# Attention in a fused attention and MLP kernel: from half-group steps to whole groups, prepared two ahead

## The chip, the cores and the metric

One Trainium2 chip, one core. The metric is the device time of one execution in microseconds (us), lower is better; the time before is the median of three runs.

## The reference

Attention over 2 sequences, 8 heads, 768 positions, head size 64. A query sees the first 4 keys (the sink) and the last 128. The result, 1536 tokens by 512, goes through two MLPs.

```python
scores = scale * np.matmul(q, k.transpose(0, 1, 3, 2))
keep = is_sink | in_window            # pos < n_sink, or 0 <= rel < window
scores = np.where(keep, scores, -1000000000.0)
a = np.exp(scores - np.max(scores, axis=-1, keepdims=True))
a = a / (np.sum(a, axis=-1, keepdims=True) + 1e-09)
x = np.matmul(a, v)                   # then heads side by side
x = (silu(x @ w_gate) * (x @ w_val)) @ w_out          # MLP 1: 512 -> 1536 -> 512
h = x @ w_in                                           # MLP 2: 512 -> 2048 -> 512
x = (np.maximum(h, 0) + alpha * np.minimum(h, 0)) @ w2_out
```

The MLP weights arrive as 64-bit floats.

## The kernel before

**Groups.** Attention is cut into 24 groups: one sequence, one pair of heads, two blocks of 128 queries (`i0` = 0, 2 or 4; `Group`, L143). Eight groups fill one token pass of 512 columns, so there are three passes. The first eight groups have `i0` = 0 and need no sink columns; the other sixteen do. A group goes through these steps:

- `load`, `load_v` (L164, L176): DMAs of its keys, queries and values, and of 32 sink keys when `i0` = 2, all issued by SyncE's queue (SP).
- `prep` (L189): TensorE (PE) transposes two or three key blocks (L206), the sink keys (L208) and two query blocks (L217) into PSUM; ScalarE (ACT) copies them to the tile `th` (L199), in two copies for a sink group.
- `scores(t)` for each of its two query blocks (L235): score matmuls (L256); VectorE (DVE) merges the two window blocks into one (L260) and adds the mask and takes the row maximum (L262, read back as `nb`); ACT does the exponential with a row sum (L266).
- `norm` (L279): DVE takes the reciprocal of the sums (L282, L283), GpSimd (POOL) multiplies (L291, L311).
- `flip(t)` (L313): PE transposes the probabilities (L323, L336); ACT (L327, L337) or DVE (L329) copies them out.
- `values` (L339): matmuls with the values (L354) and the sink values (L359); ACT and DVE split the result in two halves `xh`, `xl` (L823, L824).

**Weights.** `Stream` (L537) loads one 128-wide strip of weights at a time (512 KB, `w_raw`, 2 buffers) and converts it: ACT reads the high words (`w_m`, L574), DVE does three integer operations (L576, L579, L582) into `w`, ACT writes the upper part `wh` (L591), DVE the lower `wl` (L592). There are 68 strips. 13 converted strips have a place during attention, 6 more after it. A strip is loaded when one before it has been converted.

**MLP 1** runs in units of one chunk (4 strips each of gate, value and out) and one token pass: matmuls `pg`, `pv` (L642 to L644) and `po` (L706 to L708), all 128x128 by 128x512, 144 in a unit. The first two units (chunk 0, passes 0 and 1) are woven into the attention of the later passes; the third and all others come after it.

**Order.** The code is emitted in the order of `attention` (L366): half a group per step, the values three steps later (`LAG`), `prep` one group ahead. A scheduler of the language then sets the final order on each engine at build time; each engine runs its list strictly in that order. All PSUM tiles share 8 banks.

Of the kernel before, what the change touches and what calls it, by code (L numbers as in the profile page):

```python
# [7 lines left out]
F32 = mybir.dt.float32  # L8
# [28 lines left out]
RB = 2  # L37
LAG = 3
VB = 4
ORDER = ((0, 3), (1, 2), (4, 5))  # L40
TICK0 = 14
# [91 lines left out]
def attention_pools(nc, tc, ctx, g):  # L133
    for nm, bufs in (("raw_p", 2), ("tr_p", 2), ("pr_p", 3), ("pt_p", 2), ("st_p", 4)):
        setattr(g, nm, ctx.enter_context(tc.tile_pool(name=nm, bufs=bufs)))
    g.nb = g.const.tile([P, B * H * NQ], F32, name="nb")
    g.wsum = g.const.tile([P, NW], F32, name="wsum")
    g.ksr = g.const.tile([NPAIR * SINK, 2, D], F32, name="ksr")
    g.vsr = g.const.tile([4 * SINK, NPAIR, NG, 2 * D], F32, name="vsr")
    nc.gpsimd.memset(g.vsr, 0.0)  # L140


class Group:  # L143
    def __init__(self, nc, g, q, k, v, b, hp, i0, put, cs, blk):
# [3 lines left out]
        self.rows = slice(hp * SINK, (hp + 1) * SINK)  # L148
# [5 lines left out]
        self.kpos, c = [], 0  # L154
        for t in range(self.nk):
            self.kpos.append(c)
            c += P
            if t == 1 and self.sink:
                self.spos = c
                c += SINK  # L160
        self.kw = c
        self.whole = True

    def load(self):  # L164
        nc, p = self.nc, self.g.raw_p
        b, h0, j0, nk, i0 = self.b, self.h0, self.j0, self.nk, self.i0
        qr = p.tile([P, NG, 2, D], F32, tag="qr", name="qr")
        kr = p.tile([P, NK, 2, D], F32, tag="kr", name="kr")
        for e in range(2):
            nc.sync.dma_start(out=kr[:, :nk, e], in_=self.k[b, h0 + e, j0 * P:(j0 + nk) * P, :].rearrange("(t p) d -> p t d", p=P))  # L170
            nc.sync.dma_start(out=qr[:, :, e], in_=self.q[b, h0 + e, i0 * P:(i0 + NG) * P, :].rearrange("(t p) d -> p t d", p=P))
        if i0 == NG:
            nc.sync.dma_start(out=self.g.ksr[self.rows], in_=self.k[b, h0:h0 + 2, 0:SINK, :].rearrange("h p d -> p h d"))
# [15 lines left out]
    def prep(self):  # L189
        nc, g, nk = self.nc, self.g, self.nk  # L190
        n = NK * P + SINK + NG * P
        if self.whole:
            self.th = g.tr_p.tile([P, n], F32, tag="th", name="th")
        else:
            self.th = g.tr_p.tile([P, n], F32R, tag="th", name="th")
            self.tl = g.tr_p.tile([P, n], F32R, tag="tl", name="tl")

        def evac(ps, c, w):
            nc.scalar.activation(self.th[:, c:c + w], ps[:, :w], AF.Copy)  # L199
            if not self.whole:  # L200
                nc.vector.tensor_tensor(out=self.tl[:, c:c + w], in0=ps[:, :w], in1=self.th[:, c:c + w], op=ALU.subtract)

        self.qpos = q0 = self.kw
        ps = g.ps_t.tile([P, 512], F32, tag="ps", name="ps_k")
        for t in range(nk):
            nc.tensor.transpose(ps[:, self.kpos[t]:self.kpos[t] + P], self.kr[:, t], g.ident)  # L206
        if self.sink:
            nc.tensor.transpose(  # L208
                ps[:, self.spos:self.spos + SINK], g.ksr[self.rows].rearrange("p e d -> p (e d)"), g.ident[self.rows, self.rows]
            )  # L210
        if self.kw + NG * P > 512:
            evac(ps, 0, self.kw)
            yield 110 * nk + 60
            ps = g.ps_t.tile([P, 512], F32, tag="ps", name="ps_q")
            q0 = 0
        for t in range(NG):
            nc.tensor.transpose(ps[:, q0 + t * P:q0 + (t + 1) * P], self.qr[:, t], g.ident)  # L217
        if q0:
            evac(ps, 0, q0 + NG * P)
        else:  # L220
            evac(ps, self.kw, NG * P)
        yield 110 * NG
# [12 lines left out]
    def scores(self, t):  # L235
# [13 lines left out]
        qs, ks = slice(self.qpos + t * P, self.qpos + (t + 1) * P), slice(lo, lo + first + w)  # L249
        terms = [(self.th, self.th)]  # L250
        if not self.whole:
            terms += [(self.tl, self.th), (self.th, self.tl)]
        for z, (qx, kx) in enumerate(terms):
            for e in range(2):
                r = slice(e * D, (e + 1) * D)
                nc.tensor.matmul(pss[e][:, :first + w], qx[r, qs], kx[r, ks], start=(z == 0), stop=(z == len(terms) - 1))  # L256
# [108 lines left out]

def attention(groups, begin):  # L366
# [11 lines left out]
    for c in groups[0].prep():  # L378
        yield c, None
    for x in range(NG * n + LAG + 1):  # L380
        gi, t = divmod(x, NG)
        if x < NG * n:
            groups[gi].scores(t)
            yield 600, None
        y = x - LAG - 1
        if y >= 0 and y % NG == NG - 1:
            for c in groups[y // NG].values():
                yield c, None
            yield 0, groups[y // NG]
        y = x - LAG  # L390
        if 0 <= y < NG * n:
            groups[y // NG].flip(y % NG)
            yield 500, None
        if x < NG * n and t == NG - 1:
            groups[gi].norm()
            yield 0, None
        if t == 0:
            stage("load", gi + 2)
            if gi + 1 < n:
                for c in groups[gi + 1].prep():  # L400
                    yield c, None
        else:
            stage("load_v", gi + 1)
# [133 lines left out]
class Stream:  # L537
# [23 lines left out]
    def convert(self):  # L561
# [4 lines left out]
        w32 = g.raw_w.tile([P, KD * P], F32, tag="w32", name="w32")  # L566
# [351 lines left out]
```

## Time and profile before

| | us |
|---|---|
| median of three runs (lowest, highest) | 701.21 (700.1, 701.56) |
| the profiled execution's own time | 704.09 |
| its span, first to last instruction | 702.3 |
| PE busy (share) | 672.9 (96%) |
| PE weight loads busy | 530.2 (75%) |
| DVE busy | 407.9 (58%) |
| ACT busy | 304.1 (43%) |
| POOL busy | 44.0 (6%) |

PE matmuls overlap one another, so a busy PE may still run below its pace; the distance from one start to the next tells more. Shares are averages over stages that differ: the first 56 us hold attention alone, up to 202 us attention and MLP are woven, and after that there is MLP alone.

### The profile page before, as it was taken

How to read it: one execution, taken by the hardware profiler on the slowest of the kernel's cores; microseconds unless marked ns; L12 is line 12 of the kernel's file. 1: busy time of each engine (PE TensorE's matmuls, PEld its weight loads, DVE VectorE, ACT ScalarE, POOL GpSimd, SP SyncE). 2: the span in 40 equal slices, each digit the busy share in tenths (PEclk: the TensorE clock that was granted, in tenths of full speed). 3: DMA queues.
4: the chain of work that ended last, by engine and by line, in shares of the span. 5: the costliest groups of instructions: out<-in, count | busy, mean ns of one | idle time of the engine just before them, and what ended most of it. 6: DMA issues, size and time to landing. Idle time of an engine off the chain costs nothing.

```text
span 702.3 us, 9084 instructions
## 1 busy us (share of the span) xinstructions
PE 672.9 (96%) x3217; PEld 530.2 (75%) x3217; DVE 407.9 (58%) x926; ACT 304.1 (43%) x694; POOL 44.0 (6%) x74
## 2 busy tenths in 40 slices
PE   5788999999989989999999999999999999999996
PEld 3455667676778868888888888888888888888885
DVE  4588894755458684257842469945854743343432
ACT  4787665665436452224432245545622431123320
POOL 2232121211100000000000000000000000000000
PEclk9999999999999999999999999999999999999999
DMA  5586453421013442013320022411410000000111
GB/s 98 138 214 183 140 153 76 109 55 33 1 54 126 123 148 90 1 59 122 121 60 1 0 91 91 128 52 31 149 61 0 31 0 1 1 0 1 60 61 64
DMA packets 78820, 51.40 MB, mean 73 GB/s; under 512 B 53168, under 2 KB 73648, under 8 KB 78768
## 3 DMA queue, kind: packets, MB, share of 16 engines
q1 hardware_dynamic: 78768, 50.75, 25.2%
q8 instruction: 27, 0.44, 0.3%
q14 instruction: 25, 0.20, 0.1%
HBM read 47.59 MB, written 3.15 MB: 72 GB/s over the span
## 4 chain that ended last, share of the span: by engine, by line
PE 81%; DVE 7%; DMA 5%; ACT 3%; issue 2%; SPq 1%; POOL 0%; DVEq 0%; ACTq 0%; POOLq 0%
PE ph L643 6%; PE ph L644 6%; PE pf L763 6%; PE pf L764 6%; PE pf L762 6%; PE ph L642 6%; PE po L706 4%; PE po L708 4%; PE po L707 4%; PE pv L642 4%; PE pv L643 4%; PE pv L644 4%; PE pg L642 4%; PE pg L643 3%; PE pg L644 3%; PE ps_s L256 3%
## 5 line engine op out<-in xcount | busy, mean ns | idle before, releaser
L655 ACT ACTIVATE hh<-hid 128x512 fp32r<-128x512 f32 x84 | 52.9, 630 | 65.9 <-DVE hid L690 34.4
L656 DVE TENSOR_TENSOR hl<-hid,hh 128x512 fp32r<-128x512 f32 x84 | 58.3, 694 | 31.8 <-ACT hh L655 31.4
L642 PE MATMUL ph<-yh,wh 128*128 128x512 f32 x192 | 74.8, 389 | 0.0
L644 PE MATMUL ph<-yh,wl 128*128 128x512 f32 x192 | 74.7, 389 | 0.0
L643 PE MATMUL ph<-yl,wh 128*128 128x512 f32 x192 | 74.7, 389 | 0.0
L762 PE MATMUL pf<-wh,hh 128*128 128x512 f32 x192 | 74.7, 389 | 0.0
L763 PE MATMUL pf<-wl,hh 128*128 128x512 f32 x192 | 74.7, 389 | 0.0
L764 PE MATMUL pf<-wh,hl 128*128 128x512 f32 x192 | 71.8, 389 | 0.0
L744 ACT ACTIVATE neg<-ph,sal 128x512 f32<-128x512 f32 x48 | 32.8, 684 | 88.6 <-PE ph L644 88.6
L591 ACT ACTIVATE wh<-w 128x512 fp32r<-128x512 f32 x68 | 42.8, 630 | 59.2 <-PE pg L643 17.4
L592 DVE TENSOR_TENSOR wl<-w,wh 128x512 fp32r<-128x512 f32 x68 | 47.6, 700 | 28.6 <-ACT wh L591 26.3
L706 PE MATMUL po<-hh,wh 128*128 128x512 f32 x144 | 57.5, 401 | 2.4 <-ACT hh L655 2.4
L642 PE MATMUL pv<-xh,wh 128*128 128x512 f32 x144 | 57.4, 398 | 0.7 <-ACT pr L266 0.7
L642 PE MATMUL pg<-xh,wh 128*128 128x512 f32 x144 | 56.9, 398 | 0.4 <-ACT pr L266 0.4
L574 ACT ACTIVATE w_m<-w_raw 128x512 f32<-128x512 f32 x52 | 34.8, 669 | 51.4 <-DMA w_raw<-in_moe_w_in 17.8
L643 PE MATMUL pv<-xl,wh 128*128 128x512 f32 x144 | 56.8, 395 | 0.0
L644 PE MATMUL pv<-xh,wl 128*128 128x512 f32 x144 | 56.8, 394 | 0.0
L707 PE MATMUL po<-hh,wl 128*128 128x512 f32 x144 | 56.7, 394 | 0.0
L643 PE MATMUL pg<-xl,wh 128*128 128x512 f32 x144 | 56.3, 391 | 0.0
L644 PE MATMUL pg<-xh,wl 128*128 128x512 f32 x144 | 56.2, 390 | 0.0
L746 DVE SCALAR_TENSOR_TENSOR hid<-ph,sig,neg 128x512 f32<-128x512 f32 x48 | 36.0, 749 | 31.6 <-ACT neg L744 31.5
L708 PE MATMUL po<-hl,wh 128*128 128x512 f32 x144 | 53.7, 396 | 0.0
(118 smaller groups left out, 1208.6 us busy)
## 6 DMA issues: line engine op xcount, KB each, us to landing
w_raw<-in_moe_w_out SPq DMA_DIRECT2D x28, 512.0 KB, 3.2
w_raw<-in_moe_w_in SPq DMA_DIRECT2D x16, 512.0 KB, 3.7
w_raw<-in_moe_w_gate SPq DMA_DIRECT2D x12, 512.0 KB, 3.9
w_raw<-in_moe_w_val SPq DMA_DIRECT2D x12, 512.0 KB, 3.9
qr<-in_q SPq DMA_DIRECT2D x48, 64.0 KB, 2.4
kr<-in_k SPq DMA_DIRECT2D x32, 96.0 KB, 2.6
vr<-in_v SPq DMA_DIRECT2D x32, 96.0 KB, 2.4
out<-acc SPq DMA_DIRECT2D x12, 256.0 KB, 2.1
```

Of the source, the lines that this page charges most:

```text
L592: nc.vector.tensor_tensor(out=wl, in0=w32, in1=wh, op=ALU.subtract)
L642: nc.tensor.matmul(ps, wh[:, c], xh[:, kk], start=(kk == 0), stop=False)
L643: nc.tensor.matmul(ps, wh[:, c], xl[:, kk], start=False, stop=False)
L644: nc.tensor.matmul(ps, wl[:, c], xh[:, kk], start=False, stop=(kk == KD - 1))
L655: nc.scalar.activation(hh, hid, AF.Copy)
L656: nc.vector.tensor_tensor(out=hl, in0=hid, in1=hh, op=ALU.subtract)
L706: nc.tensor.matmul(ps, wh[:, mc], hh, start=(x == 0), stop=False)
L707: nc.tensor.matmul(ps, wl[:, mc], hh, start=False, stop=False)
L708: nc.tensor.matmul(ps, wh[:, mc], hl, start=False, stop=(x == CHUNK - 1))
L762: nc.tensor.matmul(ps, hh[:, ts], wh, start=(x == 0), stop=False)
L763: nc.tensor.matmul(ps, hh[:, ts], wl, start=False, stop=False)
L764: nc.tensor.matmul(ps, hl[:, ts], wh, start=False, stop=(x == CHUNK - 1))
```

## The change

- **Whole groups.** `attention` now takes one group per step: both score blocks, then the values of the group two before, then both flips of the group before, the norm, and the `prep` of the group two ahead. `tr_p` has 3 buffers for `th`.
- **Sink keys.** Those of a sequence are loaded in 4 DMAs, transposed once on PE (L360 of the new file), copied out by ACT to `kst`, and copied by POOL into each group's `th` (L193): 2 transposes where there were 16.
- **Shared key block.** In the passes where a group with `i0` = 4 follows its `i0` = 2 neighbour, its first key block is neither loaded nor transposed again; POOL copies the transposed block (L196). This holds for 8 groups. The other sink groups transpose that block apart (L199). All sink groups fill `th` with one strided copy of four blocks (L207).
- **Conversion in place.** The integer operations write back to `w_m`; `w` is gone, and `w_raw` has 3 buffers.
- **Order of work.** The first eight groups go by sequence; only two strips are asked for ahead of the first unit (`EARLY`) instead of by a cost count; chunk 0 asks for all four gate strips before the four value strips and gives its first eight places back together.

```diff
-RB = 2
-LAG = 3
+RB = 3
-TICK0 = 14
+EARLY = 2
...
-    for nm, bufs in (("raw_p", 2), ("tr_p", 2), ("pr_p", 3), ("pt_p", 2), ("st_p", 4)):
+    for nm, bufs in (("raw_p", 2), ("tr_p", 3), ("pr_p", 3), ("pt_p", 2), ("st_p", 4)):
...
     def prep(self):
+        self.th = th = g.tr_p.tile([P, P + 4 * KW], F32, tag="th", name="th")
+        if self.sink:
+            hp = self.hp
+            nc.gpsimd.tensor_copy(th[:, self.spos:self.spos + SINK], g.kst[self.b][:, hp * SINK:(hp + 1) * SINK])
+            if self.before is not None:
+                o = self.before.kpos[2]
+                nc.gpsimd.tensor_copy(th[:, 0:P], self.before.th[:, o:o + P])
+            else:
+                ps = g.ps_t.tile([P, 512], F32, tag="ps", name="ps_k0")
+                nc.tensor.transpose(ps[:, 0:P], self.kr[:, 0], g.ident)
+                nc.scalar.activation(th[:, 0:P], ps[:, 0:P], AF.Copy)
+        ps = g.ps_t.tile([P, 512], F32, tag="ps", name="ps_k")
+        k0 = self.nk - 2
+        for x, src in enumerate([self.kr[:, k0], self.kr[:, k0 + 1], self.qr[:, 0], self.qr[:, 1]]):
+            nc.tensor.transpose(ps[:, x * P:(x + 1) * P], src, g.ident)
+        if self.sink:
+            dst = th[:, P:].rearrange("p (x w) -> p x w", x=4)[:, :, 0:P]
+            nc.scalar.activation(dst, ps.rearrange("p (x w) -> p x w", x=4), AF.Copy)
...
+def sink_keys(nc, g, b):
+    ps = g.ps_t.tile([P, 512], F32, tag="ps", name="ps_ks")
+    nc.tensor.transpose(ps[:, :P], g.ksr[b], g.ident)
+    nc.scalar.activation(g.kst[b], ps[:, :P], AF.Copy)
...
+    for x in range(n + 2):
+        if x < n:
+            for t in range(NG):
+                groups[x].scores(t)
+            yield 1200, None
+        if x >= 2:
+            for c in groups[x - 2].values():
                 yield c, None
+            yield 0, groups[x - 2]
+        if 1 <= x <= n:
+            for t in range(NG):
+                groups[x - 1].flip(t)
+            yield 1000, None
+        if x < n:
+            groups[x].norm()
             yield 0, None
+        if x + 2 < n:
+            for c in groups[x + 2].prep():
+                yield c, None
+        stage("load", x + 3)
+        stage("load_v", x + 1)
+        if x < B:
+            begin[2](x)
+        elif x < 2 * B:
+            begin[3](x - B)
...
-        w32 = g.raw_w.tile([P, KD * P], F32, tag="w32", name="w32")
         m = g.raw_w.tile([P, KD * P], F32, tag="m", name="w_m")
-        mi, wi = m.bitcast(I32), w32.bitcast(I32)
+        mi, mu = m.bitcast(I32), m.bitcast(U32)
...
-            if done < per:
-                if cost >= TICK0 * 1000:
-                    cost = 0
+            if done < per:
+                if c == 1000 and st.n_conv < EARLY:
                     st.tick()
```

PE, one sink group in the stretch of attention without MLP matmuls, before: scores, values, sink values, flip, scores, flip, transposes.

```order
L256 MATMUL ps_s<-th 128x288 x2
L354 MATMUL xp<-pt,vr 64x256 x2
L354 MATMUL xp<-pt,vr 64x128 x4
L359 MATMUL xp<-pts,vsr 128x128 x2
L323 MATMUL ps_p<-ident,pr 128x128 x2
L256 MATMUL ps_s<-th 128x288 x2
L323 MATMUL ps_p<-ident,pr 128x128 x2
L336 MATMUL ps_p_1578<-ident,sk 128x128
L206 MATMUL ps_k<-ident,kr 128x128 x3
L208 MATMUL ps_k<-ident,ksr 128x32
L217 MATMUL ps_q<-ident,qr 128x128 x2
```

PE, the same place in the change (a group that shares its key block):

```order
L240 MATMUL ps_s<-th 128x288 x4
L338 MATMUL xp<-pt,vr 64x256 x2
L338 MATMUL xp<-pt,vr 64x128 x4
L343 MATMUL xp<-pts,vsr 128x128 x2
L307 MATMUL ps_p<-ident,pr 128x128 x4
L320 MATMUL ps_p_1324<-ident,sk 128x128
L204 MATMUL ps_k<-ident,kr 128x128 x2
L204 MATMUL ps_k<-ident,qr 128x128 x2
```

The scores of a group stand together, so do its flips, and six transposes have become four (five where L199 is in the list). In the new order six such groups (the 13th to the 18th) follow one another with no MLP matmul between them, and the first unit's 144 matmuls are woven with two groups; before, the first unit was woven with four to five groups, and three and a half stood alone.

DVE, one group at that place, before (L262 ISA is the masked maximum and its read-back):

```order
L282 TENSOR_SCALAR rinv<-ssum 128x4
L283 RECIPROCAL rinv<-rinv 128x4
L329 TENSOR_TENSOR pt<-ps_p,tri 128x2x256
L824 TENSOR_TENSOR xl<-xp,xh 128x256
L260 COPY_PREDICATED ps_s<-above,ps_s 128x128 x2
L329 TENSOR_TENSOR pt<-ps_p,tri 128x2x256
L262 ISA ps_s,nb<-ps_s,mask_a 128x160
L262 ISA nb 128x1
L262 ISA ps_s,nb<-ps_s,mask_a 128x160
L262 ISA nb 128x1
L260 COPY_PREDICATED ps_s<-above,ps_s 128x128
```

DVE, the same in the change, from the reciprocal to the next scores:

```order
L266 TENSOR_SCALAR rinv<-ssum 128x4
L267 RECIPROCAL rinv<-rinv 128x4
L313 TENSOR_TENSOR pt<-ps_p,tri 128x2x256 x2
L830 TENSOR_TENSOR xl<-xp,xh 128x256
L244 COPY_PREDICATED ps_s<-above,ps_s 128x128 x2
L246 ISA ps_s,nb<-ps_s,mask_a 128x160
L246 ISA nb 128x1
L246 ISA ps_s,nb<-ps_s,mask_a 128x160
L246 ISA nb 128x1
L244 COPY_PREDICATED ps_s<-above,ps_s 128x128 x2
```

The instructions are the same; both copies of a group's flips now stand behind its reciprocal, where one stood between the scores.

SP's queue in the first stage, around the first weight strips, before (five groups are loaded ahead of them):

```order
L170 DMA kr<-in_k 128x2x64 x2
L171 DMA qr<-in_q 128x2x64 x2
L181 DMA vr<-in_v 128x2x64 x2
L554 DMA w_raw<-in_moe_w_gate 128x4x256 x2
L170 DMA kr<-in_k 128x2x64
```

The same in the change (four groups and the sink keys ahead):

```order
L171 DMA kr<-in_k 128x2x64 x2
L172 DMA qr<-in_q 128x2x64 x2
L180 DMA vr<-in_v 128x2x64 x2
L352 DMA ksr<-in_k 32x2x64 x4
L555 DMA w_raw<-in_moe_w_gate 128x4x256 x3
L171 DMA kr<-in_k 128x2x64
```

Three strips instead of two are asked for at once, two DMAs earlier, and the keys of the fifth group stand behind them.

## Rows read from the trace of the kernel before

**Rows 1.** Windows: stretch, then its length and each engine's busy time, granted clock, DMA.

```profile
0.00:55.65 55.65, 40.21 (x243) 24.63 (x243) 36.72 (x161) 38.14 (x129) 16.59 (x27) 0.97 0.65 151
55.65:135.12 79.47, 76.73 (x436) 53.04 (x434) 59.97 (x188) 52.38 (x152) 16.65 (x27) 0.98 0.51 135
120.19:135.12 14.93, 14.87 (x114) 9.62 (x113) 11.50 (x50) 9.89 (x37) 3.08 (x6) 1.00 0.46 104
135.12:201.98 66.86, 64.06 (x385) 46.10 (x383) 33.57 (x118) 33.70 (x92) 10.79 (x21) 1.00 0.13 29
201.98:237.00 35.02, 35.02 (x158) 29.00 (x156) 26.89 (x48) 18.41 (x39) 0.00 (x0) 1.00 0.37 120
```

**Rows 2.** Timeline of ACT, first stage: start, length, instruction, [idle before, releaser].

```profile
22.61 0.66 ACT L574 ACTIVATE w_m<-w_raw 128x512 f32<-128x512 f32 x1 [3.58 <-DMA w_raw<-in_moe_w_gate]
38.33 0.68 ACT L574 ACTIVATE w_m<-w_raw 128x512 f32<-128x512 f32 x1 [0.77 <-DMA w_raw<-in_moe_w_val]
```

**Rows 3.** Groups by shape, first 205 us: busy us, mean ns of one | idle.

```profile
L199 ACT ACTIVATE th<-ps_k 128x416 f32<-128x416 f32 x16 | 8.3, 517 | 1.1 <-PE ps_k L208 1.1
L199 ACT ACTIVATE th<-ps_q 128x256 f32<-128x256 f32 x16 | 6.2, 389 | 0.8 <-PE ps_q L217 0.8
L199 ACT ACTIVATE th<-ps_k 128x512 f32<-128x512 f32 x8 | 4.8, 603 | 4.1 <-PE ps_k L217 4.1
L311 POOL TENSOR_TENSOR sk<-pr,rinv 128x64 f32<-128x64 f32 x32 | 11.4, 376 | 0.0
masks.py:197 POOL MEMSET ident<- 128x128 f32 x1 | 0.2, 204 | 0.0
```

**Rows 4.** Timeline of PE, one sink group alone, from its scores to the next.

```profile
122.23 0.76 PE L256 MATMUL ps_s<-th 64*128 64x288 f32 x4
124.48 0.38 PE L323 MATMUL ps_p<-ident,pr 128*128 128x128 f32 x2
124.80 0.76 PE L256 MATMUL ps_s<-th 64*128 64x288 f32 x4
125.48 0.44 PE L323 MATMUL ps_p<-ident,pr 128*128 128x128 f32 x2
125.87 0.49 PE L206 MATMUL ps_k<-ident,kr 128*128 128x128 f32 x3
126.83 0.76 PE L256 MATMUL ps_s<-th 64*128 64x288 f32 x4
```

**Rows 5.** Timeline of PE, first stage: four transposes, then the next scores.

```profile
34.47 0.38 PE L206 MATMUL ps_k<-ident,kr 128*128 128x128 f32 x2
35.00 0.70 PE L256 MATMUL ps_s<-th 64*128 64x256 f32 x4
```

**Rows 6.** Timeline of DVE in the group of rows 4: last read-back, then the reciprocal.

```profile
124.21 0.14 DVE L262 DVE_READ_ACCUMULATOR2_ANT nb<- 128x1 f32 x1
125.04 0.17 DVE L282 TENSOR_SCALAR rinv<-ssum 128x4 f32<-128x4 f32 x1 [0.68 <-ACT pr L266]
```

**Rows 7.** Timeline of PE after attention: four 128x512 matmuls apart by three instructions.

```profile
256.49 0.39 PE L706 MATMUL po<-hh,wh 128*128 128x512 f32 x1
257.17 0.39 PE L706 MATMUL po<-hh,wh 128*128 128x512 f32 x1
```

**Rows 8.** Timeline of PE in the first woven unit; the window right after.

```profile
70.21 0.87 PE L354 MATMUL xp<-pt,vr 128*64 128x256 f32 x8 [2.12 <-DVE pt L329]
71.00:75.56 4.56, 4.56 (x14) 3.31 (x13) 3.33 (x11) 2.06 (x7) 0.00 (x0) 0.63 0.49 154
```

**Rows 9.** After attention: one PE wait, an ACT row before it, the window after.

```profile
PE po L706 <- ACT hh L655: 2.4, 1, 2.4
255.68 0.66 ACT L574 ACTIVATE w_m<-w_raw 128x512 f32<-128x512 f32 x1 [1.86 <-DMA w_raw<-in_moe_w_gate]
262.50:280.00 17.50, 17.50 (x71) 14.26 (x71) 8.55 (x15) 5.36 (x12) 0.00 (x0) 0.90 0.27 91
```

More of the change, by code (lines that the diff above doesn't have):

```diff
@@ L137, in attention_pools @@
     g.wsum = g.const.tile([P, NW], F32, name="wsum")
-    g.ksr = g.const.tile([NPAIR * SINK, 2, D], F32, name="ksr")
+    g.ksr = [g.const.tile([NPAIR * SINK, 2 * D], F32, name="ksr") for _ in range(B)]
+    g.kst = [g.const.tile([P, NPAIR * SINK], F32, name="kst") for _ in range(B)]
     g.vsr = g.const.tile([4 * SINK, NPAIR, NG, 2 * D], F32, name="vsr")
@@ L153, in __init__ @@
         self.off = 1 if i0 == 0 else 0
[L154 to L162, printed above, removed]
+        self.before = None
+        if self.sink:
+            self.kpos = [0, P, P + KW]
+            self.spos = 2 * P
+            self.qpos = [P + 2 * KW, P + 3 * KW]
+        else:
+            self.kpos = [0, P]
+            self.qpos = [2 * P, 3 * P]
     def load(self):
         nc, p = self.nc, self.g.raw_p
-        b, h0, j0, nk, i0 = self.b, self.h0, self.j0, self.nk, self.i0
+        b, h0, i0 = self.b, self.h0, self.i0
+        n0 = 1 if self.before is not None else 0
+        j0, nk = self.j0 + n0, self.nk - n0
+        self.n0 = n0
         qr = p.tile([P, NG, 2, D], F32, tag="qr", name="qr")
@@ L189, in prep @@
     def prep(self):
[L190 to L193, printed above, removed]
-        else:
[L195 to L215, printed above, removed]
@@ L248, in scores @@
             pss.append(ps)
[L249 to L256, printed above, removed]
+        qs, ks = slice(self.qpos[t], self.qpos[t] + P), slice(lo, lo + first + w)
+        for e in range(2):
+            r = slice(e * D, (e + 1) * D)
+            nc.tensor.matmul(pss[e][:, :first + w], self.th[r, qs], self.th[r, ks], start=True, stop=True)
         for e in range(2):
@@ L363, in values, with sink_load @@
         yield 700
+def sink_load(nc, g, k, b):
+    for hp in range(NPAIR):
+        nc.sync.dma_start(
+            out=g.ksr[b][hp * SINK:(hp + 1) * SINK].rearrange("p (e d) -> p e d", e=2),
+            in_=k[b, 2 * hp:2 * hp + 2, 0:SINK, :].rearrange("h p d -> p h d"),
+        )
+def sink_keys(nc, g, b):
+    ps = g.ps_t.tile([P, 512], F32, tag="ps", name="ps_ks")
+    nc.tensor.transpose(ps[:, :P], g.ksr[b], g.ident)
+    nc.scalar.activation(g.kst[b], ps[:, :P], AF.Copy)
 def attention(groups, begin):
@@ L377, in attention @@
     begin[1]()
[L378 to L387, printed above, removed]
-                yield c, None
[L389 to L395, printed above, removed]
-            yield 0, None
[L397 to L403, printed above, removed]
+    for x in range(2):
+        for c in groups[x].prep():
+            yield c, None
+    stage("load", 2)
+    for x in range(n + 2):
[5 more added lines that the diff above has]
+            for c in groups[x - 2].values():
+                yield c, None
+            yield 0, groups[x - 2]
[5 more added lines that the diff above has]
+            groups[x].norm()
+            yield 0, None
+        if x + 2 < n:
+            for c in groups[x + 2].prep():
+                yield c, None
+        stage("load", x + 3)
[4 more added lines that the diff above has]
+            begin[3](x - B)
 def verdict(nc, g):
@@ L667, in unit, with at @@
         w0 = self.base + c * 3 * CHUNK
+        def at(kind, x):
+            return w0 + (kind * CHUNK + x if c == 0 else 2 * (x - x % 2) + 2 * kind + x % 2)
         xh, xl = self.xs[b]
@@ L692, in unit @@
                 hid_of.append((hh, hl))
-                if last and r == 1:
-                    st.done(4)
+                if last and r == 1 and (c or x + 2 == CHUNK):
+                    st.done(4 if c else 2 * CHUNK)
                 yield
@@ L831, in fast @@
         ]
+        for x, y in zip(groups, groups[1:]):
+            if x.i0 == NG and y.i0 == 2 * NG and (x.b, x.hp) == (y.b, y.hp):
+                y.before = x
+        groups[:2 * NPAIR] = groups[0:2 * NPAIR:2] + groups[1:2 * NPAIR:2]
         per = len(groups) // NPASS
-        ready, skip = [], []
+        ready = []
         done = cost = 0
-        for c, grp in attention(groups, (begin_a, begin_b)):
+        for c, grp in attention(groups, (begin_a, begin_b, lambda b: sink_load(nc, g, k, b), lambda b: sink_keys(nc, g, b))):
             cost += c
@@ L838, in fast @@
                 done += 1
-                if done % per == 0 and done < len(groups):
-                    b = done // per - 1
-                    skip.append((0, b))
-                    ready.append(m1.unit(0, b))
+                if done in (per, 2 * per):
+                    ready.append(m1.unit(0, done // per - 1))
             if done < per:
-                if cost >= TICK0 * 1000:
-                    cost = 0
+                if c == 1000 and st.n_conv < EARLY:
                     st.tick()
@@ L851, in fast @@
                 st.tick()
-    while ready and next(ready[0], ready) is ready:
-        ready.pop(0)
     for u in ready:
```

41 lines of the change are left out of this document (20 added, 21 removed).

## The prediction

> **What bounds the kernel now.** I read the windows by stage first, to see which engine is full where. Up to 55.65 us, when the first MLP matmul runs, PE is busy 40.21 us and ACT 38.14 of 55.65 [rows 1]; the timeline of ACT adds stalls of 3.58 and 0.77 us on weight strips that had not landed [rows 2]. Here PE has slack and the start of the MLP hangs on ACT: it copies transposes and probabilities, takes exponentials and converts strips. From 55.65 to 201.98 us PE is the bound: busy 76.73 of 79.47 and 64.06 of 66.86 us, and in the 15 us of attention alone, 120.19 to 135.12, it works 14.87 of 14.93 us at granted clock 1.00 [rows 1]. After 201.98 us there is only MLP, and PE again has no gap (35.02 of 35.02) [rows 1].
>
> For prices I went to PE's timeline. Four 128x512 matmuls end to end go from 256.49 to 257.17 for three, so one takes 0.227 us [rows 7], and a unit of 144 takes 32.6 us. A sink group alone goes from its scores at 122.23 to the next scores at 126.83: 4.60 us, of which the six transposes, from 125.87 on, are 0.96 [rows 4].
>
> The second woven stretch can now be split: 79.47 = 32.6 (one unit) + 39.1 (8.5 groups of 4.60) + 7.8 us left for waits and slow clock. I counted the 8.5 groups from the order of the scores. Of the 7.8, one wait is 2.12 us (values waiting for a flip that DVE copies out), and right behind it the clock is 0.63 for 4.56 us; 14 matmuls at 0.227 would have been 3.2, so 1.4 more is clock [rows 8].
>
> After 201.98 us one place loses time: a wait of 2.4 us of the out-matmuls for the hidden tile, behind ACT, which had itself waited 1.86 us for a gate strip; then the granted clock is 0.90 for 17.5 us [rows 9], a tenth of it, 1.75 us. Together 4.2 us.
>
> **The change part by part.**
>
> *Transposes (16 sink groups).* PE loses three instructions per group, or two where the shared block is not at hand. Four transposes up to the next scores took 0.53 us (34.47 to 35.00) [rows 5], against 0.96 for six: 0.43 saved with four; five, at a quarter of 0.53 more, save 0.30. Eight groups have four, eight five: 8 x 0.43 + 8 x 0.30 = 5.8 us. The two new sink transposes cost 2 x 0.27, where PE has slack. But when PE gets quicker, DVE is next: its order within a group is closed by its own dependences. It is busy 11.50 us in 14.93, which are 3.25 groups: 3.5 us each [rows 1], and it must wait, as now, from the last read-back (124.21) to the reciprocal (125.04), 0.68 idle, for the exponential [rows 6]. That is 4.2 us per group, as much as PE's 4.60 - 0.43 = 4.17. I take 0.35 per group, 16 x 0.35 = **-5.6 us**. Ends: -6.9 (all sixteen at 0.43) and 0 (DVE's chain as long as 4.60).
>
> *Flips and scores brought together.* The two flips, which now stand from 124.48 to 124.80 and from 125.48 to 125.87 with scores between [rows 4], become one row of five. The same instructions run; I count nothing for the missing switches. What it does to waits is in the next term.
>
> *Waits in the first woven unit.* Groups prepared two ahead, and flips a full step ahead of the values, take the reason from waits such as the 2.12 us one [rows 8]: the copied flip is then older by about half a group. Against it, the first unit is now woven with two groups instead of four to five, so it needs conversions faster. I let a third of the 7.8 go: **-2.4 us**. Ends: -7.8 (all) and +2.1 (one more wait like the one shown).
>
> *First stage.* ACT gains and loses. Copies out of a sink group become one of 512 columns at 0.603 instead of 0.517 + 0.389 [rows 3], 0.3 us saved; three such groups are prepared before the first unit, but groups without a shared block pay a further copy, bounded by 0.39 for 256 columns, so all this is about zero. The sink keys' copy is at most 0.39, and the order has one more first conversion (`w_m`) before the unit, 0.68 at ACT [rows 2], so ACT gets about 1.1 us more work. For that, strips: the order of SP puts the first three strips two DMAs earlier, and with three buffers the third doesn't wait for a conversion. The stalls of 3.58 and 0.77 us [rows 2] should shrink by some 2.6. Net **-1.5 us**. Ends: -4.2 (stalls gone, nothing added) and +4.6 (stalls as before, 1.1 more work, and the keys of the fifth group, now behind one strip more, late by its 3.5 us: 512 KB at the stage's 151 GB/s [rows 1]).
>
> *MLP alone.* The third raw buffer lets a strip be on its way while two are being converted. With two, ACT stood 1.86 us for a gate strip; this put the hidden tile late by 2.4 and the clock down [rows 9]. Of the 4.2 us I take away 2.5: **-2.5 us**; the rest stays because DVE, with 26.89 of 35.02 us busy [rows 1], is a queue in which a conversion can also stand. Ends: -4.2 and +2.0 (a wait of the same kind elsewhere: the conversion in place holds `w_m` until DVE has written the lower part, and ACT, with the silu and hidden tiles queued behind `w_m`, waits for that).
>
> *Costed at nothing.* POOL's 24 copies: their price is between a memset of 128x128 at 0.204 and a product of 128x64 at 0.376 [rows 3], 5 to 9 us in all; POOL is busy 3.08 of 14.93 us [rows 1], and a group's tile is filled two groups ahead. Bare of this cover one copy delays a group by at most 0.4, 16 x 0.4 = 6 us. Eight shared blocks spare 16 key loads' worth of queue; SP has room. The order of the first eight groups and the way places are returned move nothing that PE waits for: 19 places are there, and chunk 0 uses 12.
>
> *Sum.* -5.6 - 2.4 - 1.5 - 2.5 = -12.0 us. The profiled execution took 704.09 (span 702.3), 2.9 above the median; the difference should hold for either, so 701.2 - 12.0 = **689.2 us**.
>
> **The rivals.**
>
> 1. *The packed unit starves.* The order puts 144 matmuls of the first unit between two groups where there were four to five. Demand there by rows: DVE 26.89 x 32.6/35.02 = 25.0 plus 2 x 3.5 = 32 us, ACT 17.1 plus 2 x 3.0 = 23 us, in 41 us of PE [rows 1]. On average it fits, but each strip goes through DMA, ACT, DVE, ACT, DVE in turn, and both engines also carry groups. For it: the 2.12 us wait occurred on DVE at just this place [rows 8]. Against: seven strips (one more than before) are under conversion ahead of the unit. Then waits stay as they were, the first stage gains nothing, and MLP alone nothing: 701.2 - 5.6 = 695.6 us.
>
> 2. *The change doesn't do what it says.* Transposes that are removed were not the bound: a group alone stays at 4.60 because the chain scores, merge, maximum, exponential, reciprocal, flip, copy sets it, not PE's amount of work, and the strips arrive no sooner. For: DVE's 4.2 us is close to 4.60, and it needs no more than a POOL copy or a bank of PSUM that comes free late to close the gap. Against: PE idles 0.06 of 14.93 us there [rows 1]. Time: 700 to 702, no change.
>
> 3. *Slower: the clock falls in the attention alone.* Six groups, not three and a half, now follow one another without MLP matmuls, and PE has pauses there if DVE sets the pace. Should the granted clock go to 1.2 GHz, a group of 4.25 takes between 1.4 times (the stretch at 0.63: 4.56 for 3.2) [rows 8] and twice as long, +1.7 to +4.2, about +3; six groups +18: 707 us. It decides from four cold groups on (4 x 3 = the whole gain). For: five flips and four transposes now stand in one row. Against: 15 us of the same work ran at clock 1.00, with three flips' and six transposes in a row [rows 1, 4]. On this the Trainium skill, in "TensorE: Matmul & The Clock Gate", section "Part 4: PE-mode transpose", says that a transpose does not count as PE work for the clock as a matmul does. By that rule alone the row of nine would be where the clock falls; the trace does not agree so far, since rows of nine such instructions stood at 1.00.
>
> **How the numbers follow.** The forecast has a chance of 0.55, and its own range is 684 to 694. Rival 1 has 0.25 (694 to 698), rival 2 0.09 (700 to 702), rival 3 0.08 (703 to 715); 0.03 is for other ways, of either sign. What a measurement of this kernel can tell from no change is about 0.2%, 1.4 us. Faster: 0.55 + 0.25 + 0.03 = 0.83; the same 0.06, most of rival 2; slower 0.11, the rest of it, rival 3 and half the others. The range from 683.5 to 698 takes in the forecast and rival 1 and leaves out rivals 2 and 3 and the far ends of the terms.
>
> **What would show it.** In the profile of the changed kernel: a sink group alone takes 4.2 to 4.3 us from scores to scores on PE (4.60 would be rival 2, more with a clock below 1.00 rival 3); the first MLP matmul comes at about 54 us, and ACT's waits for strips before it add up to less than 2 us; the first woven unit has waits of about 5 us (8 would be rival 1); the 2.4 us wait of the out-matmuls for the hidden tile is gone or halved and the clock behind it is 1.00; POOL's copies have a mean of 0.2 to 0.4 us, and no PE row waits for POOL. I am wrong if the gain lies in other stages than these, if groups take 4.60, or if a wait of ACT for `w_m` stands in the chain.

## The result

| | before | after |
|---|---|---|
| median, us (runs) | 700.67 (4) | 690.89 (4) |
| ratio, 95% interval | | 0.9861 (0.9844 to 0.9878) |
| the profiled execution's own time | 704.09 | 690.96 |
| A: start to first `pg` matmul | 55.65 | 54.55 |
| B: to the first `pg` of the second unit | 79.47 | 73.81 |
| C: to the end of attention (first `pg` of the third unit) | 66.86 | 64.73 |
| D: from there to PE's last instruction | 494.31 | 490.04 |

The change saves 9.8 us (forecast 12.0; 690.9 us where 689.2 was forecast). One of the twelve executions of the kernel before with three raw buffers, used below, took 2315.39 us; it is left out of that kernel's median and ratio. Stages A to D are read from the starts of PE's instructions; between the two profiles they differ by 1.1 + 5.7 + 2.1 + 4.3 = 13.2 us. That is 3.4 more than the medians: the profiled execution of before lies 3.4 us above its median, that of the change lies at it.

The windows of the changed kernel by stage (columns as in [rows 1]), the last being the first 35 us of D:

```profile
0.00:54.55 54.55, 38.35 (x241) 24.30 (x241) 36.64 (x158) 37.96 (x125) 19.34 (x34) 0.94 0.63 148
54.55:128.36 73.81, 69.75 (x419) 51.67 (x418) 58.80 (x187) 49.17 (x144) 18.60 (x39) 1.00 0.57 150
128.36:193.06 64.70, 62.55 (x380) 46.18 (x378) 33.60 (x122) 31.02 (x92) 12.54 (x26) 1.00 0.13 30
193.06:228.08 35.02, 35.02 (x157) 29.02 (x156) 31.80 (x57) 24.10 (x51) 0.00 (x0) 1.00 0.51 158
```

Against [rows 1], PE's busy time in B fell by 7.0 us, at clock 1.00 instead of 0.98, while its idle time rose from 2.7 to 4.1. In D PE has no gap at all, ACT's first 35 us there hold 24.10 us of work instead of 18.41, and the wait of 2.4 us with the clock of 0.90 behind it [rows 9] is gone.

PE's timeline of a sink group alone, from scores to scores, which answers to [rows 4], early and late in that stretch:

```profile
102.58 1.24 PE L240 MATMUL ps_s<-th 64*128 64x288 f32 x8
103.76 1.09 PE L338 MATMUL xp<-pt,vr 128*64 128x256 f32 x12
...
105.32 0.60 PE L307 MATMUL ps_p<-ident,pr 128*128 128x128 f32 x4
...
105.87 0.27 PE L199 MATMUL ps_k<-ident,kr 128*128 128x128 f32 x1
...
106.51 1.51 PE L240 MATMUL ps_s<-th 64*128 64x288 f32 x8
...
110.07 0.38 PE L204 MATMUL ps_k<-ident,kr 128*128 128x128 f32 x2
...
110.60 1.39 PE L240 MATMUL ps_s<-th 64*128 64x288 f32 x8
112.46 1.09 PE L338 MATMUL xp<-pt,vr 128*64 128x256 f32 x12 [0.47 <-DVE pt L313]
113.48 0.71 PE L343 MATMUL xp<-pts,vsr 128*128 128x128 f32 x4
114.03 0.60 PE L307 MATMUL ps_p<-ident,pr 128*128 128x128 f32 x4
114.57 0.27 PE L199 MATMUL ps_k<-ident,kr 128*128 128x128 f32 x1
115.21 2.00 PE L240 MATMUL ps_s<-th 64*128 64x288 f32 x8
```

The first two take 3.93 and 4.09 us; the three from 110.60 on take 4.6 each, as before. DVE's timeline of the same stretch shows the idle time that closes the loop, once in every group, as in [rows 6]:

```profile
110.85 0.17 DVE L266 TENSOR_SCALAR rinv<-ssum 128x4 f32<-128x4 f32 x1 [0.78 <-ACT pr L250]
...
111.15 1.26 DVE L313 TENSOR_TENSOR pt<-ps_p,tri 128x512 f32<-128x512 f32 x2
...
115.45 0.17 DVE L266 TENSOR_SCALAR rinv<-ssum 128x4 f32<-128x4 f32 x1 [0.78 <-ACT pr L250]
```

Both copies of the flips wait behind the reciprocal, and that waits for the exponential; PE's values then wait 0.47 us for the copies. So what PE saved became idle time in these three groups.

### The profile page after: what moved, and what is told of

It is laid out like the page before. It is cut to its first block, busy times and chain, and to the rows that moved or that the text cites. A ratio compares the mean times of both kernels' runs of the same rounds, so it can differ in the third digit from the quotient of the medians.

```text
span 689.2 us, 9053 instructions
## 1 busy us (share of the span) xinstructions
PE 660.7 (96%) x3195; PEld 527.6 (77%) x3195; DVE 405.7 (59%) x926; ACT 301.4 (44%) x686; POOL 50.5 (7%) x98
## 4 chain that ended last, share of the span: by engine, by line
PE 86%; DVE 5%; ACT 3%; DMA 3%; issue 1%; SPq 1%; POOL 0%; DVEq 0%; ACTq 0%; POOLq 0%
PE ph L646 6%; PE pf L770 6%; PE ph L644 6%; PE pf L768 6%; PE pf L769 6%; PE ph L645 6%; PE po L712 5%; PE po L714 5%; PE po L713 5%; PE pg L644 4%; PE pv L644 4%; PE pg L645 4%; PE pv L646 4%; PE pg L646 4%; PE pv L645 4%; PE ps_s L240 2%
## 5 line engine op out<-in xcount | busy, mean ns | idle before, releaser
L592 ACT ACTIVATE wh<-w_m 128x512 fp32r<-128x512 f32 x68 | 42.7, 631 | 52.0 <-DVE w_m L583 18.4
L593 DVE TENSOR_TENSOR wl<-w_m,wh 128x512 fp32r<-128x512 f32 x68 | 48.1, 710 | 24.5 <-ACT wh L592 23.9
L775 DVE TENSOR_TENSOR acc<-pf,acc 128x512 f32<-128x512 f32 x36 | 23.2, 686 | 50.5 <-PE pf L770 50.5
```

What stands on the lines that cost most here:

```text
L593: nc.vector.tensor_tensor(out=wl, in0=w32, in1=wh, op=ALU.subtract)
```

## The experiments

The results in one table: stages are those of each kernel's profile, intervals are of the ratio to before on the same chip; kernels whose intervals overlap are not told apart by their medians. `w_m` counts the conversions begun in A.

| kernel | median, us | ratio (95%) | A | B | C | D | `w_m` in A |
|---|---|---|---|---|---|---|---|
| change | 690.89 | 0.9861 (0.9844 to 0.9878) | 54.55 | 73.81 | 64.73 | 490.04 | 5 |
| before again | 705.08 (one time) | | 56.53 | 79.89 | 66.84 | 494.08 | 6 |
| two raw buffers | 698.96 | 0.9987 (0.9969 to 1.0004) | 60.22 | 74.11 | 64.72 | 492.06 | 8 |
| 32 more transposes | 693.94 | 0.9903 (0.9875 to 0.9931) | 53.77 | 76.67 | 66.05 | 490.04 | 5 |
| no 1e-9 | 690.74 | 0.9859 (0.9831 to 0.9888) | 52.46 | 75.80 | 64.72 | 490.04 | 5 |
| before, three raw buffers | 704.91 | 1.0055 (1.0033 to 1.0077) | 63.41 | 77.17 | 66.81 | 490.03 | 9 |
| half-group steps | 696.14 | 0.9925 (0.9904 to 0.9947) | 58.32 | 75.17 | 65.00 | 490.04 | 8 |
| no shared block | 691.81 | 0.9862 (0.9835 to 0.9889) | 53.87 | 77.09 | 64.43 | 490.03 | 5 |
| sink keys later | 703.13 | 1.0021 (1.0006 to 1.0036) | 70.39 | 69.06 | 64.72 | 490.04 | 14 |
| EARLY = 0 | 696.49 | 0.9928 (0.9907 to 0.9949) | 56.22 | 78.36 | 64.73 | 490.03 | 2 |
| EARLY = 1 | 689.41 | 0.9830 (0.9808 to 0.9853) | 51.97 | 76.34 | 64.73 | 490.03 | 4 |
| EARLY = 5 | 689.41 | 0.9842 (0.9818 to 0.9867) | 55.81 | 71.15 | 64.70 | 490.05 | 8 |
| EARLY = 5, no 1e-9 | 688.69 | 0.9833 (0.9812 to 0.9853) | 55.78 | 70.16 | 64.71 | 490.03 | 8 |

**The kernel before once more.** No edit.

> The kernel before, unchanged, profiled once more. Theory C: of the profiled execution of before, some 3 us (704.09 against a median near 701) belonged to that execution alone; this one takes 700 to 701.5 us, the stretch after attention does not show the 2.4 us wait of the out-matmuls with clock 0.90 behind it, or shows it smaller, and the stage from the end of attention to the end is 490 to 492 us long instead of 494.3. Rival: the wait and the low clock are part of the kernel and stand here again, the stage is 494 us, and the median gain of the change lies where the two profiles differ by stage.

Theory C fell: the profiled execution is long again, and the wait of 2.4 us [rows 9] is there again, 2.1 us long. PE's timeline of that kernel, D:

```profile
263.25 0.79 PE L706 MATMUL po<-hh,wh 128*128 128x512 f32 x1 [2.13 <-ACT hh L655]
```

So profiles of before agree with each other to 1 us, and lie 3 to 5 us above the medians of its timed runs (700.3 to 701.3 in all comparisons). The timed runs themselves spread from 698.1 to 704.8 us, and the granted clock goes with them: 0.992 to 0.997 in those below 700.2, 0.988 to 0.993 in those above 703. The two profiled executions, at 0.991 and 0.988, are like the long end of this spread.

**Two raw buffers in the change.**

```diff
-RB = 3
+RB = 2
```

> The changed kernel with two raw buffers instead of three. Theory A (the third buffer is worth what the prediction gave it, 2.5 us in the MLP stage and part of 1.5 us in the first stage): 2.5 to 4 us slower than the change, 693.4 to 695, with waits of the out-matmuls for the hidden tile back after attention. Rival: strips land early enough either way once attention is over, and the first unit gets its strips in time: within 1 us of 690.9.

Eight us, twice what theory A allowed: 2.0 in D, as expected, but 5.7 in A. ACT's timeline and PE's in that kernel show one of the places:

```profile
46.99 0.66 ACT L575 ACTIVATE w_m<-w_raw 128x512 f32<-128x512 f32 x1 [2.06 <-DMA w_raw<-in_moe_w_val]
...
47.65 0.58 ACT L311 ACTIVATE pt<-ps_p 128x512 f32<-128x512 f32 x1
```

```profile
48.28 0.87 PE L338 MATMUL xp<-pt,vr 128*64 128x256 f32 x8 [2.15 <-ACT pt L311]
```

ACT stands in order before a strip that has not landed; the copy of the flips is queued behind it, and PE's values wait as long. A also holds eight conversions here instead of five; what the rest of the 5.7 is was not taken apart.

**More transposes.** In `prep` of a sink group, two of the four transposes are issued twice:

```diff
             nc.tensor.transpose(ps[:, x * P:(x + 1) * P], src, g.ident)
+            if self.sink and x < 2:
+                nc.tensor.transpose(ps[:, x * P:(x + 1) * P], src, g.ident)
```

> The changed kernel with two of the transposes of every sink group issued twice (the first result is overwritten): 32 more PE instructions of 0.11 us, 3.5 us of PE work and nothing else. Theory A (PE sets the time of every sink group, as the prediction's term of 16 groups says): +3.5 us, 694.4, a group alone goes from 4.6 to 4.8 us. Theory B (DVE's chain sets the groups that stand alone; the change left PE with slack there): the groups alone stay at 4.6, only the ten to eleven woven with MLP matmuls pay, +2 to +2.4 us, 693.0 to 693.3. Rival to both (waits, not work, set the woven ones too): within 1 us.

**No addition of 1e-9.**

```diff
-        nc.vector.tensor_scalar(out=rinv, in0=self.ssum, scalar1=EPS, scalar2=None, op0=ALU.add)
-        nc.vector.reciprocal(out=rinv, in_=rinv)
+        nc.vector.reciprocal(out=rinv, in_=self.ssum)
```

> The changed kernel without the addition of 1e-9 to the row sums ahead of the reciprocal (one DVE instruction of 0.17 us, 0.20 to the next, in every group). Theory B (DVE's chain sets the groups alone, 4.60 us each): these take 4.40, five of them 1.0 us less in all, 689.9. Theory A (PE sets them): nothing, 690.9 within 0.4, groups alone stay at 4.6.

The two belong together. PE's timelines from scores to scores, first with more transposes (4.83 us, line numbers moved by two), then without the 1e-9 (4.40 us):

```profile
112.21 1.35 PE L242 MATMUL ps_s<-th 64*128 64x288 f32 x8
...
117.04 1.90 PE L242 MATMUL ps_s<-th 64*128 64x288 f32 x8
```

```profile
111.33 1.39 PE L240 MATMUL ps_s<-th 64*128 64x288 f32 x8
...
115.73 1.79 PE L240 MATMUL ps_s<-th 64*128 64x288 f32 x8
```

PE's extra 0.22 us shows in a group alone, and so does DVE's missing 0.20; over the five groups alone they come to 0.9 and 0.8 us. So neither engine by itself is the bound in the groups that take 4.6: one chain runs through both, scores, merge and maximum, exponential, reciprocal, copies, values, flips, transposes. As a whole, the transposes cost 3.05 us (0.095 each), between the two theories; the interval, some 2 us either way, can't separate them, the group alone does. Leaving out the 1e-9 gains nothing as a whole: A is 2.1 us shorter and the groups alone 0.8 (not the 1.0 expected, as the first of them gains nothing), but B as a whole is 2.0 longer. Where it loses that is shown under EARLY below.

**Three raw buffers in the kernel before.** `RB = 3` there, nothing else.

> The kernel before with three raw buffers and nothing else. Theory D (the third buffer carries most of the change's gain by itself: taking it from the change cost 8.1 us, of which 5.7 stood before the first MLP matmul and 2.0 after attention): 5 to 8 us faster than before, 692.5 to 695.5. Rival E (it is worth that only together with the change's order, in which strips are asked for three at a time early and keys stand behind them; in the order of before it mends only the wait after attention): 1 to 3 us faster, 697.5 to 699.5.

Both fell: it is slower. D is 490.03, so the third buffer alone removes the loss of D. But A is 7.8 us longer. Windows of A, that kernel and then the change with sink keys later (below), the second line its worst ten us:

```profile
0.00:63.41 63.41, 48.16 (x242) 28.60 (x243) 42.76 (x168) 42.28 (x137) 17.64 (x26) 0.84 0.67 164
```

```profile
0.00:70.39 70.39, 50.30 (x240) 31.33 (x240) 54.11 (x185) 48.19 (x150) 20.17 (x33) 0.77 0.73 185
50.00:60.00 10.00, 8.41 (x37) 5.34 (x37) 9.51 (x26) 8.82 (x29) 4.43 (x6) 0.50 0.86 235
```

The scheduler, given the buffer, set nine conversions into A instead of six; the granted clock fell to 0.84, and 242 PE instructions were busy for 48.16 us where 243 had taken 40.21 [rows 1]. Whether the conversions brought the clock down is not shown.

**Half-group steps in the change.** `attention` alternates the two query blocks again; the sum of the step costs stays:

```diff
-            for t in range(NG):
-                groups[x].scores(t)
-            yield 1200, None
+            groups[gi].scores(t)
+            yield 600, None
...
-            for t in range(NG):
-                groups[x - 1].flip(t)
-            yield 1000, None
+            groups[y // NG].flip(y % NG)
+            yield (1000 if y % NG else 0), None
```

> The changed kernel with half-group steps again: scores and flips of a group's two query blocks alternate as in the kernel before, the values three steps later, groups still prepared two ahead, all other edits kept. Theory A (bringing scores and flips together gains nothing by itself; the gain is fewer transposes and the strips): within 1.5 us of the change, 689.5 to 692.5. Rival F (whole groups take waits away in the woven units): 3 us or more slower, 694 or above, with waits of the values for flips that ACT or DVE copies back in the woven units.

Rival F by its size, 5.2 us, but for the larger part not by its place: between the profiles 3.8 are in A and 1.6 in B and C. From PE's waits over the whole kernel (total, times, longest):

```profile
PE xp L338 <- ACT pt L311: 6.0, 8, 1.4
```

The values wait eight times for flips that ACT copies, all in A; in the change no such wait is listed. Eight conversions stand in A here, too, so part of the 3.8 may be theirs. Its groups alone take 4.65 to 4.88 us each; none is as short as the first two of the change (3.93 and 4.09).

**No shared key block.**

```diff
-                y.before = x
+                y.before = None
```

> The changed kernel with the shared key block off: eight groups load and transpose their first key block again (8 PE transposes of 0.11 us, 8 ACT copies of 0.27 us, 16 larger key loads), and 8 copies leave POOL. Theory A (PE work counts): +0.9 to +1.5 us, 691.8 to 692.4. Rival (POOL's copies stand in the path of the probabilities on POOL, since each group alone has the product by the reciprocal behind them): 0 to 2 us faster, 689 to 690.9.

+0.9 us in the median, the lower end of theory A; the intervals overlap, so the sign is not secured.

**Sink keys later.**

```diff
-        if x < B:
-            begin[2](x)
-        elif x < 2 * B:
-            begin[3](x - B)
+        if x in (2, 10):
+            begin[2](x // 10)
+        elif x in (5, 13):
+            begin[3](x // 13)
```

> The changed kernel with the sink keys of each sequence loaded and transposed later: loads after the third and eleventh group instead of the first two, transposes three groups behind. In the changed kernel PE waits 4.2 us for the sink keys of the second sequence, whose loads stand behind a strip in the first stage. Theory G (that wait delays the first stage): the first MLP matmul comes 2 to 4 us earlier than 54.5 and the whole is 1.5 to 4 us faster, 687 to 689.4. Rival H (ACT and the strips set the first stage and the packed first unit; PE has slack there): within 1 us of 690.9, since the first unit then waits for its strips instead.

Neither: 12 us slower. The order built from it holds 14 conversions in A, DVE is busy 54.11 of 70.39 us, and the clock is 0.77, for ten us at 0.50, the lower level of 1.2 GHz (lines above). The unit gives back 4.8 in B. So the run says nothing on the wait of 4.2 us that it was to remove; it shows how far a small move of queue entries can move this schedule.

**How many strips ahead: EARLY = 0, 1, 5.**

```diff
-EARLY = 2
+EARLY = 0
```

> The changed kernel with EARLY = 0: no strip is asked for ahead of the first unit; the order has one conversion before the eighth group's result. Theory I: first stage 7 to 9 us shorter, 46 to 48 us, the whole not faster, since the first unit then needs its strips one after the other, each on its way through DMA and two engines, which PE has no work to hide: packed unit 5 to 12 us longer, the whole 688 to 694. Rival J: exactly the gain of the first stage is lost, 690.9 within 1.

> The changed kernel with EARLY = 1: in the order built from it four strip conversions stand on ACT before the eighth group's result, instead of five. Theory I (the length of the first stage is set by the conversions that stand in it: over the kernels so far, 5 conversions 52.5 to 54.6 us, 6 55.7 to 56.5, 8 58.3 to 60.2, 9 63.4, 14 70.4, so about 1.8 us each, and the first woven unit gives little of it back): first MLP matmul 1.5 to 2 us earlier, the whole 0.5 to 2 us faster than the change, 689 to 690.4. Rival J (fewer strips ready, the first unit waits for them by as much as the stage is shorter): 690.9 within 0.5, the gain of the first stage lost in the first woven unit. Rival H (other things set the stage): first matmul where it was.

> The changed kernel with EARLY = 5: eight to nine conversions before the eighth group's result instead of five, nothing else edited. Theory I: first MLP matmul at 59 to 61 us (3 to 3.5 conversions at 1.8), the first woven unit gives back at most the 2 to 3 us that PE waits there, the whole 2 to 5 us slower than the change, 693 to 696. Rival J (strips ready early save the unit as much): 690.9 within 1. Rival K (the length of the first stage followed the lower clock and not the conversions): first matmul within 1.5 us of 54.5 unless the clock in 20 to 60 us is below 0.9.

Theory I fell with EARLY = 5, where nothing but the number of strips was edited: three more conversions lengthen A by only 1.3 us (0.4 each, not 1.8), which is rival K's sign, B gets 2.7 shorter, and the median is 1.5 us lower, though the intervals overlap. The 1.8 of the other kernels was not the conversions' own price.

With EARLY = 1 the median is 1.5 us lower, too, with overlapping intervals, but the profiled execution (690.95) is level with the change's: A is 2.6 shorter and B 2.5 longer, as rival J said. The run without the 1e-9 shows the same pair, 2.1 and 2.0. One wait of PE at the start of B, in the change, without the 1e-9 and with EARLY = 1:

```profile
57.59 0.44 PE L307 MATMUL ps_p<-ident,pr 128*128 128x128 f32 x2 [0.48 <-ACT pr L250]
57.64 0.44 PE L306 MATMUL ps_p<-ident,pr 128*128 128x128 f32 x2 [2.62 <-ACT pr L250]
57.59 0.44 PE L307 MATMUL ps_p<-ident,pr 128*128 128x128 f32 x2 [3.07 <-ACT pr L250]
```

ACT's timeline just before, in the same order; the exponential (`pr`) stands right behind this strip:

```profile
56.41 0.66 ACT L575 ACTIVATE w_m<-w_raw 128x512 f32<-128x512 f32 x1 [2.46 <-DMA w_raw<-in_moe_w_val]
56.47 0.66 ACT L574 ACTIVATE w_m<-w_raw 128x512 f32<-128x512 f32 x1 [4.61 <-DMA w_raw<-in_moe_w_val]
56.42 0.66 ACT L575 ACTIVATE w_m<-w_raw 128x512 f32<-128x512 f32 x1 [5.05 <-DMA w_raw<-in_moe_w_val]
```

and the six us behind it, in the change and without the 1e-9:

```profile
58.00:64.00 6.00, 5.23 (x24) 4.20 (x24) 5.84 (x15) 3.78 (x12) 0.49 (x1) 1.00 0.71 165
58.00:64.00 6.00, 5.35 (x13) 3.98 (x13) 5.85 (x14) 3.81 (x12) 2.55 (x3) 0.50 0.83 197
```

The value strip lands at 56.4 us in all three, however early PE has come to its first MLP matmul. What A won is spent waiting for it, and behind the longer wait the clock stands at 0.50 (0.52 with EARLY = 1) instead of 1.00. So a shorter A was worth nothing in these profiles.

With EARLY = 0 PE stands before its unit's first matmul, which ends A, and again within the unit; both theories fell, since A is 1.7 us longer and the whole 5.6. PE's timeline:

```profile
56.22 0.80 PE L644 MATMUL pg<-xh,wh 128*128 128x512 f32 x1 [6.64 <-ACT wh L592]
69.48 0.80 PE L644 MATMUL pv<-xh,wh 128*128 128x512 f32 x1 [4.43 <-ACT wh L592]
```

and the ten us around the first of these waits:

```profile
50.00:60.00 10.00, 3.78 (x11) 3.08 (x12) 6.70 (x15) 5.28 (x17) 2.84 (x4) 0.57 0.98 267
```

That is rival 1 of the prediction made true: PE waits 11 us for converted strips. In the kernels with EARLY = 1, 2 and 5 no wait of PE in B is for a strip of its own.

**EARLY = 5 and no 1e-9 together.**

> The changed kernel with EARLY = 5 and without the addition of 1e-9 to the row sums. Theory L (with the strips ready the first woven unit does not wait for them, so both edits count: 1.4 us from the strips, 1.0 us from five groups alone at 4.40 instead of 4.60): 688.0 to 689.0, faster than either. Rival M (the first stage and the first woven unit move by more than that from any edit, through waits of ACT for strips and through the clock, as when the same edit alone lost in the unit what it won before it): 689 to 691, no gain over EARLY = 5 alone, though the groups alone take 4.40.

688.69 us, within theory L: B is 1.0 shorter than with EARLY = 5 alone, three groups alone at 4.4 instead of 4.6 and the first two at 3.9. It has the lowest median of the study, though its interval overlaps those of the change and of EARLY = 1 and 5.

## Why the prediction was right, and where its terms were off

*The sum.* 12.0 forecast, 9.8 measured in the medians, 13.2 between the profiles. The step that failed is "the difference should hold for either". Two profiles of before agree, both lie above its medians, and both are like the longest of its timed runs, in time and in clock, so the stages that I priced are those of a long execution. Where a shorter one loses less is not shown. One thing fits: the profiled executions of the kernel before with three buffers (705.43 against a median of 704.91) and of the change with two (698.93 against 698.96) lie near their medians, and their D is shorter, so it may be D's wait and the clock behind it, which a timed run of before would then have smaller. This was only argued. Two slips in the working change little: the stalls of [rows 2] add up to 4.35, not 4.2, and the 0.03 of other ways is counted whole among the faster and half among the slower.

*MLP alone, -2.5.* Right mechanism, shown by the third buffer alone in the kernel before (D 494.31 to 490.03) and by taking it away (+2.0). Between the profiles the gain is 4.3, all of the 4.2 that I had read from [rows 9].

*First stage, -1.5.* Measured -1.1, but as a difference of large parts. I priced one conversion more in A; there was one less, 5 against 6. And the stage does not hang on ACT as I had it. ACT's waits for strips fell from 5.4 us to 0.4, twice the 2.6 that I counted on, but PE's waits for keys and sink keys rose from 4.9 to 14.4. The waits in A (total, times, longest) of ACT before and in the change, then of PE before (of PE in the change: below):

```profile
ACT w_m L574 <- DMA w_raw<-in_moe_w_gate: 4.6, 3, 3.6
ACT w_m L574 <- DMA w_raw<-in_moe_w_val: 0.8, 1, 0.8
ACT w_m L575 <- DMA w_raw<-in_moe_w_gate: 0.4, 1, 0.4
PE ps_k L206 <- DMA kr<-in_k: 4.9, 2, 4.4
```

The third buffer was worth 5.7 us here inside the change, and cost 7.8 inside the kernel before, so it has no price by itself. My range for this stage (-4.2 to +4.6) was too narrow for what single edits did (51.97 to 70.39 us).

*Transposes and waits, -5.6 and -2.4.* B and C together: -7.8, forecast -8.0 (the border between them moved by half a group, so they are not read apart). That the sum fits is luck, because the terms behind it are off both ways. PE's own price of the transposes was right: the 0.96 of six [rows 4] became 0.53 with four (110.07 to 110.60) and 0.64 with five (105.87 to 106.51); only the count in words was one too high, as PE loses two instructions per group or one. But the groups alone gain nothing after the second one: 4.6 us where I had 4.25. The step that failed is DVE's "4.2 us": I added its busy 3.5 and its wait 0.68 [rows 1, 6], but in the change the busy time between two reciprocals is 3.82 and the wait 0.78, 4.60 together. The 3.5 was an average over a window in which DVE first waits 2.43 us for scores; between two reciprocals of the kernel before (125.04 and 129.82) DVE, the third engine listed, was busy 3.99 us of 4.78:

```profile
125.04:129.82 4.78, 4.78 (x39) 3.03 (x37) 3.99 (x18) 3.17 (x13) 1.54 (x3) 1.00 0.38 83
```

That was rival 2's mechanism, and it held in that stretch alone. The woven groups gained more than 0.35 each. A group with 24 MLP matmuls in C, from its scores to the next, before and then in the change:

```profile
154.50 0.76 PE L256 MATMUL ps_s<-th 64*128 64x288 f32 x4
...
164.86 0.76 PE L256 MATMUL ps_s<-th 64*128 64x288 f32 x4
```

```profile
149.05 1.24 PE L240 MATMUL ps_s<-th 64*128 64x288 f32 x8
...
158.66 1.24 PE L240 MATMUL ps_s<-th 64*128 64x288 f32 x8
```

These are 10.36 and 9.61 us; the other groups of C with 24 matmuls take 10.16 to 10.51 before and 9.50 in the change. The transposes explain 0.32 of the 0.75 and the scores in one row (next term) 0.2; the rest was not taken apart. PE's waits in B, at last, did not shrink: the one of 2.12 us is gone, but the idle time grew by 1.3 us; the clock, 0.98 to 1.00 over 79 us, is worth 1.6 (an estimate: 0.02 of 79).

*Bringing flips and scores together, nothing.* This step failed, too: "I count nothing for the missing switches" put at nothing what the rows price. Eight scores in one row take 1.18 us to the next instruction (102.58 to 103.76), where four took 0.68 (124.80 to 125.48 [rows 4]) and so twice four 1.36; five flips in one row take 0.55 (105.32 to 105.87), where the two rows took 0.32 and 0.39. That is 0.35 us of PE in a group alone, as much as the transposes were counted at; the first such group, at 3.93, shows both together. Undoing it cost 5.2 us. Some of it is the conversions that the order then puts into A; how much was not separated.

*Costed at nothing.* The shared block and POOL's copies: 0.9 us at most, and no PE row waits for a copy of POOL, though the 128x128 copy takes 0.474 in the mean, above my bound of 0.376. These copies of POOL between 55 and 195 us:

```profile
L196 POOL COPY th<-th 128x128 f32<-128x128 f32 x6 | 2.8, 474 | 14.6 <-ACT th L207 14.6
```

*The rivals.* 1: PE idles 4.1 us in the whole of B; the unit starves for strips only with none ahead. 2: its mechanism held for three groups, see above. 3: in the stretch of groups alone the clock stayed at 1.00, nine transposes in a row or not:

```profile
98.00:128.36 30.36, 29.42 (x231) 21.77 (x230) 22.98 (x104) 18.58 (x77) 10.94 (x27) 1.00 0.49 114
```

The clock fell in another place, the first stage. PE's waits in A of the changed kernel (total, times, longest), and ten us windows around the second of them, which ends at 31.4 us:

```profile
PE ps_k L204 <- DMA kr<-in_k: 10.2, 4, 4.0
PE ps_ks L360 <- DMA ksr<-in_k: 4.2, 1, 4.2
```

```profile
20.00:30.00 10.00, 4.43 (x35) 2.78 (x33) 9.05 (x27) 9.40 (x33) 3.03 (x4) 0.95 0.81 190
30.00:40.00 10.00, 7.83 (x45) 4.87 (x45) 6.45 (x25) 6.79 (x25) 2.32 (x3) 0.71 0.63 157
```

From 20 to 30 us PE is busy 4.43 of ten, and the next ten stand at 0.71; with EARLY = 0 it was a wait of 6.64 us, for a strip that ACT converts, and 0.57 in the ten us around it. On this the Trainium skill, in "TensorE: Matmul & The Clock Gate", section "HAM oscillation — how this bites in real kernels", says that PE's waits for DMA between short bursts bring it back to the low clock, so that each burst starts cold. The trace agrees at the wait for the sink keys: 0.95 in the ten us with most of the wait, 0.71 in the ten behind.

## What to carry to other kernels

Work taken off the engine that is busiest counts only where no chain through the next engine closes at the same length; add that engine's busy time between two of its own waits to the wait, from one group of the trace, before pricing the gain. A buffer more has no fixed price where a scheduler sets the order: the same third buffer was worth 8 us in one program and cost 4 in the other, and the built order changed with it, so read that order before pricing. A stage made shorter gains nothing if the next one starts with a wait for something that lands at a fixed time. And a profiled execution that lies above the median is not a neutral base for a sum: hold its time and clock against the timed runs, and price what lies between.

## What the runs showed of the hardware

In the first stage the same 240 PE instructions were busy from 36.54 us (EARLY = 0) to 50.30 us (sink keys later), the longest at a mean granted clock of 0.77. Which edit moves the clock could not be told from the kernel's order. In the pairs shown it was low behind the longer waits of PE: 0.50 and 0.52 from 58 to 64 us behind waits of 2.62 and 3.07 us, 1.00 behind one of 0.48. After attention, with PE without a gap, D was 490.03 to 490.05 us in all eleven kernels with three buffers.
